# Attention, two MoE layers on one core: blocks 0 and 1 take turns with each chunk of w1 and w2, block 1's products wait in DRAM, attention's scaling moves into the masking

## The chip, the cores and the metric

One core of a Trainium2 chip. The metric is device time in microseconds of one execution; beside it stand one profiled execution and its trace.

## The reference, cut to what matters

```python
# attention: q, k, v are [4, 8, 576, 64]; heads 0-3 plain, 4-7 dilated by 4
scores = q @ k.T / sqrt(64)
scores = where(mask, scores, -1e9)          # window 32 (plain) or 128 in steps of 4 (dilated)
attn = exp(scores - max(scores)); attn = attn / (sum(attn) + 1e-9)
x = (attn @ v) as [2304 tokens, 512]
# first MoE
x = ((x @ w1) * (x @ w2)) @ w3 @ w_out      # w1, w2 [512, 1024], w3 [1024, 1024], w_out [1024, 512]
# second MoE
h = x @ w_in                                # [512, 2048]
y = (P(h) / (Q(h) + 1e-6)) @ w_out2         # P cubic, Q quadratic in h
```

The inputs of both MoE layers are float64; everything else is float32.

## The kernel before, in words

**Weights.** They come as pairs of 32-bit words (512 KB for a chunk of 128 x 512 numbers, `load`). Each chunk is decoded to float32 by one instruction of ScalarE (`scale`) and three of VectorE (`shift`, `sign`, `low_bits`). For the exact products a number is split in a high and a low part of fp32r: ScalarE rounds the high part (`high`), VectorE subtracts for the low part (`low`), and a product takes three matmuls (`SPLIT`).

**First MoE.** w3 @ w_out is made first, in two halves of 16 jobs (`w3_mm`, two matmuls of 512 columns each; "w3 job" below); its result stays as `W3o`. The 2304 tokens are eight blocks of 288 (k = 0 to 7). For block k and chunk m (0 to 7) two jobs of twelve matmuls of 288 columns make x @ w1 and x @ w2 (`l1`, e = 0 and 1), ScalarE copies the first (`l1_copy`), VectorE multiplies (`l1_mul`, the product p), ScalarE rounds p to its high part (`l1_high`) and GpSimd subtracts (`l1_low`). Eight jobs of twelve matmuls per block then multiply by W3o (`l2`). Each of the 16 chunks of w1 and w2 (two for each m) is decoded and split once, before its first l1 job; from then on all of them stay in SBUF. l1 of block 0 is thus the stage that runs while they are decoded.

**Attention.** A batch feeds two blocks and has eight groups G (four pairs of heads, two halves of the rows each). A group is a chain over the engines: scores on TensorE (`att_qk`), masking with the row maximum on VectorE (`att_mask`, six instructions, and one that scales the maxima by -0.125), six exps on ScalarE (`att_exp`), sums and reciprocal on VectorE (`att_sums`), two scalings on GpSimd (`att_norm`), transposes on TensorE (`att_pt`), copies on ScalarE (`att_pc`), the product with v on TensorE (`att_pv`), and the split into `xs` (`att_high`, `att_low`).

**Order.** All of attention and the first MoE are jobs of a planner (`Plan`). Each job has an engine, a work time, buffers and a due time; `main_jobs` writes down in which order TensorE's large jobs fall due (`PACE`, `W3_AT`), attention's groups are due some microseconds apart ahead of the first l1 job of their blocks (`GAP0`, `GAP`). The planner lists the jobs of each engine in one fixed order, and on the chip each engine takes its list in that order; an instruction that waits holds up all that stand behind it on its engine. SyncE issues all DMAs in a planned order too. PSUM has four tags of two banks: `ab` (l1), `acc` (l2, w3), `sc` (scores, second half of w3), `px` (transposes and pv). The second half of w3 needs the two `acc` banks that the first half leaves and the two `sc` banks that the last scores leave.

**Second MoE.** `phase2`, a loop written by hand. Its 32 weight chunks are decoded during the first MoE and wait in DRAM (`wd`).

Of the kernel before, what the change touches and what calls it, by code (L numbers as in the profile page):

```python
# [10 lines left out]
F32 = mybir.dt.float32  # L11
# [42 lines left out]
GAP0, GAP = 4.0, 8.0  # L54
LEAD = 20.0
W3_AT = 0
NORM_ACT = 0
PP_POOL = 0
PACE = 1.17
# [14 lines left out]
class Plan:  # L74
# [105 lines left out]
class Kern:  # L180
# [161 lines left out]
    def att_exp(self, G, h):  # L342
        pr, sm = self.pr[G], self.sm[G]
        for i in range(3 * h, 3 * h + 3):
            self.nc.scalar.activation(out=pr[:, i], in_=pr[:, i], func=AF.Exp, scale=0.125,  # L345
                                      bias=sm[:, 1, i:i + 1], accum_out=sm[:, 2, i:i + 1])

    def att_sums(self, G):
        sm = self.sm[G]
        self.nc.vector.tensor_scalar(out=sm[:, 3], in0=sm[:, 2], scalar1=1.0, scalar2=1e-9,  # L350
                                     op0=ALU.mult, op1=ALU.add)
        self.nc.vector.reciprocal(out=sm[:, 3], in_=sm[:, 3])  # L352

# [32 lines left out]
    def att_x(self, G):  # L386

        u, half = divmod(G, 2)
        b, hp = divmod(u, HP)
        if hp < HP // 2:  # L390
            return [(self.xs[2 * b + half][:, :, hp], self.xt[G][:, 0:TA])]
        sv = self.xt[G][:, 0:TA].rearrange("p (r i) -> p r i", r=2)
        return [(self.xs[2 * b + e][:, :, hp].rearrange("p w (i r) -> p w r i", r=4)
                 [:, :, 2 * half:2 * half + 2], sv[:, :, e * 72:(e + 1) * 72]) for e in range(2)]

    def att_high(self, G):
        b = G // (2 * HP)
        for k in (2 * b, 2 * b + 1):
            if k not in self.xs:
                pool = self.xs01 if k % 4 < 2 else self.xs23  # L400
                self.xs[k] = pool.tile([P, 2, KC, TA], F32R, tag=f"xs{k % 4}", bufs=1, name="xs")
        for dst, src in self.att_x(G):
            self.nc.scalar.copy(dst[:, 0], src)

    def att_low(self, G):
        for dst, src in self.att_x(G):
            self.nc.vector.tensor_tensor(out=dst[:, 1], in0=src, in1=dst[:, 0].bitcast(F32),
                                         op=ALU.subtract)
# [21 lines left out]
    def l1(self, k, m, e):  # L430
        xs, w = self.xs[k], self.w12[2 * m + e]["w"]
        t = self.ab[k, m, e] = self.bank("ab")
        n = 0
        for s in SPLIT:
            for c in range(KC):
                self.nc.tensor.matmul(t[:, 0:TA], w[:, s[0], c * P:(c + 1) * P], xs[:, s[1], c],  # L436
                                      start=n == 0, stop=n == 11)
                n += 1
# [59 lines left out]
    def phase1(self):  # L498
# [9 lines left out]
        for t in slots + [f"xs{i}" for i in range(4)]:  # L508
            bufs[t] = 1
# [12 lines left out]
        for G in range(2 * B * HP):  # L522
# [17 lines left out]
            m1 = add("DVE", 0.86, self.att_mask, G, 1, after=[qk, m0], use=[prb, smb, sc[1]])  # L540
# [3 lines left out]
            eng = "ACT" if G < NORM_ACT else "POOL"  # L544
            no = [add(eng, {"ACT": 1.2, "POOL": 0.8}[eng], self.att_norm, G, h, eng, after=[su],
                      use=[prb, smb]) for h in range(2)]
            pc = []
            for h in range(2):
# [4 lines left out]
            n = 1 if hp < HP // 2 else 2  # L553
            xn = [xsb[2 * b], xsb[2 * b + 1]]
            first = G % (2 * HP) == 0
            hi = add("ACT", 0.43 * n, self.att_high, G, after=[pv] + ([low[G - 1, "h"]] if not first else []),
                     new=xn if first else [], use=px[2:] + ([] if first else xn))
            low[G, "h"] = hi
            low[G] = add("DVE", 0.42 * n, self.att_low, G, after=[hi], use=px[2:] + xn,
                         due=due)  # L560
# [69 lines left out]
        l1s, l2s, stored = [], {}, {}  # L630
        for k in range(NA):
            b = k // 2
            lows_k = [low[G] for G in range(b * 2 * HP, (b + 1) * 2 * HP)]
            pl_lo, gbs = [], []
            for m in range(M1):
                tb = [buf("t"), buf("t")]
                mm = []
                for e in range(2):
                    ab = buf("ab")
                    mm.append((add("PE", 1.57, self.l1, k, m, e, after=lows_k + [w12[2 * m + e]] + l1s[-1:],  # L640
                                   new=[ab], use=[xsb[k], w12b[2 * m + e]], due=T["l1", k, m, e]), ab))
                    l1s.append(mm[-1][0])
                c = add("ACT", 0.42, self.l1_copy, k, m, after=[mm[0][0]], new=tb[0:1], use=[mm[0][1]],
                        due=T["l1", k, m, 1])
                mu = add("DVE", 0.42, self.l1_mul, k, m, after=[c, mm[1][0]], new=tb[1:2],
                         use=[tb[0], mm[1][1]], due=T["l1", k, m, 1] + 2)
                if m % 2 == 0:
                    gb = buf("g")
                    gbs.append(gb)
                hi = add("ACT", 0.45, self.l1_high, k, m, after=[mu], new=[gb] if m % 2 == 0 else [],  # L650
                         use=[tb[1]] + ([gb] if m % 2 else []), due=T["l1", k, m, 1] + 5)
                on_pool = k >= PP_POOL
                pl_lo.append(add("POOL" if on_pool else "DVE", 0.8 if on_pool else 0.38, self.l1_low, k, m,
                                 on_pool, after=[hi], use=[tb[1], gb], port=True))
            if k == NA - 1:
                break
# [13 lines left out]
            l1s.append(l2s[k, KC - 1])  # L670

# [34 lines left out]
    def main_jobs(self):  # L706
# [193 lines left out]
    def run(self):  # L900
        with self.pool("cpool") as self.cpool, self.pool("decp") as self.decp, \
# [3 lines left out]
            self.wd = dram.tile([2, FC, P, DM], F32, name="wd")  # L905
            self.x2d = dram.tile([2, KC, P, NT], F32, name="x2d")
# [86 lines left out]
```

## Time and profile before

| | |
|---|---|
| time, median of 3 runs | 870.48 us (869.77 to 871.95) |
| the profiled execution | 869.54 us, its span 867.8 us |
| TensorE busy in the span | 840.2 us, 97% |
| VectorE, ScalarE, GpSimd busy | 584.3, 534.0, 334.8 us |
| mean granted clock of TensorE | 0.996 of 2.4 GHz |
| DMA | 92.70 MB, mean 107 GB/s, 357 GB/s at the start |

The span runs from the first to the last instruction; the profiled time is 1.7 us more, and the median 0.9 us above the profiled time. Matmuls overlap, so a busy TensorE is not a TensorE at its peak: how long a job takes is read from the distance of its start to the next one's.

### The profile page before, as it was taken

How to read it: one execution, taken by the hardware profiler on the slowest of the kernel's cores; microseconds unless marked ns; L12 is line 12 of the kernel's file. 1: busy time of each engine (PE TensorE's matmuls, PEld its weight loads, DVE VectorE, ACT ScalarE, POOL GpSimd, SP SyncE). 2: the span in 40 equal slices, each digit the busy share in tenths (PEclk: the TensorE clock that was granted, in tenths of full speed). 3: DMA queues.
4: the chain of work that ended last, by engine and by line, in shares of the span. 5: the costliest groups of instructions: out<-in, count | busy, mean ns of one | idle time of the engine just before them, and what ended most of it. 6: DMA issues, size and time to landing. Idle time of an engine off the chain costs nothing.

```text
span 867.8 us, 14594 instructions
## 1 busy us (share of the span) xinstructions
PE 840.2 (97%) x5216; PEld 719.5 (83%) x5216; DVE 584.3 (67%) x1308; ACT 534.0 (62%) x1222; POOL 334.8 (39%) x313
## 2 busy tenths in 40 slices
PE   6989799999999999999999999999999999999998
PEld 3546599989998999989998878888888888888886
DVE  6999996776767224331214887787787877797775
ACT  5874565654566334542235877787777777787773
POOL 2220032422243222312022755565555655564443
PEclk9999999999999999999999999999999999999999
DMA  9876438585766212033225100010000100000112
GB/s 357 300 271 215 154 114 264 172 244 197 252 197 194 76 36 95 20 113 138 80 58 203 37 13 12 13 49 13 25 12 25 37 13 12 13 25 35 47 48 92
DMA packets 41737, 92.70 MB, mean 107 GB/s; under 512 B 4544, under 2 KB 12736, under 8 KB 41664
## 3 DMA queue, kind: packets, MB, share of 16 engines
q1 hardware_dynamic: 41664, 91.77, 31.7%
q8 instruction: 41, 0.67, 0.3%
q14 instruction: 32, 0.26, 0.1%
HBM read 70.39 MB, written 21.36 MB: 106 GB/s over the span
## 4 chain that ended last, share of the span: by engine, by line
PE 78%; DVE 9%; ACT 6%; DMA 4%; issue 2%; POOL 1%; SPq 0%; POOLq 0%; DVEq 0%; ACTq 0%
PE ab L436 19%; PE acc L824 11%; PE sc L824 11%; PE ab L774 11%; PE px L774 10%; PE acc L466 9%; ACT pr L345 2%; PE acc L416 2%; DVE dec L225 2%; PE sc L318 2%; PE px L383 2%; DMA words<-moe_w_in 2%; PE px L368 1%; DVE dec L236 1%; DVE dec L221 1%
## 5 line engine op out<-in xcount | busy, mean ns | idle before, releaser
L436 PE MATMUL ab<-xs,w 128*128 128x288 f32 x1536 | 216.5, 300 | 3.3 <-ACT w L243 2.8
L436 PEld LDWEIGHTS ab<-xs,w 128*128 128x128 f32 x1536 | 207.7, 190 | 8.3 <-ACT w L243 3.6
L785 POOL TENSOR_TENSOR y<-y,v 128x512 f32<-128x512 f32 x72 | 95.9, 1332 | 142.9 <-ACT y L784 142.7
L458 POOL TENSOR_TENSOR pp<-p,pp 128x288 fp32r<-128x288 f32 x64 | 55.8, 873 | 185.1 <-ACT pp L453 175.8
L361 POOL TENSOR_TENSOR pr<-pr,sm 96x384 f32<-96x384 f32 x64 | 55.2, 881 | 154.4 <-DVE sm L352 115.0
L466 PE MATMUL acc<-pp,w 128*128 128x288 f32 x768 | 110.4, 299 | 1.6 <-DVE XS L882 1.0
L824 PE MATMUL acc<-w,gg 128*128 128x512 f32 x432 | 109.8, 391 | 1.5 <-ACT r L795 1.5
L824 PE MATMUL sc<-w,gg 128*128 128x512 f32 x432 | 109.4, 390 | 0.0
L466 PEld LDWEIGHTS acc<-pp,w 128*128 128x128 f32 x768 | 103.4, 188 | 4.0 <-PE acc L466 1.2
L774 PE MATMUL ab<-XS,w 128*128 128x512 f32 (+1 forms) x480 | 105.4, 370 | 0.0
L774 PE MATMUL px<-XS,w 128*128 128x512 f32 (+1 forms) x480 | 105.3, 370 | 0.0
L811 POOL TENSOR_TENSOR gg<-t,gg 128x512 fp32r<-128x512 f32 x72 | 93.8, 1303 | 10.6 <-ACT gg L810 10.1
L774 PEld LDWEIGHTS px<-XS,w 128*128 128x128 f32 x480 | 83.9, 188 | 16.4
L774 PEld LDWEIGHTS ab<-XS,w 128*128 128x128 f32 x480 | 83.8, 188 | 16.2
L824 PEld LDWEIGHTS acc<-w,gg 128*128 128x128 f32 x432 | 80.8, 188 | 19.2 <-ACT r L795 1.9
L824 PEld LDWEIGHTS sc<-w,gg 128*128 128x128 f32 x432 | 80.9, 188 | 17.2
L446 DVE TENSOR_TENSOR p<-a_sb,ab 128x288 f32<-128x288 f32 x64 | 29.0, 453 | 88.1 <-PE ab L436 70.8
L345 ACT ACTIVATE pr<-pr,sm 96x128 f32<-96x128 f32 x192 | 74.7, 392 | 16.4 <-DVE sm L339 16.3
L802 DVE SCALAR_TENSOR_TENSOR v<-y,cs,r 128x512 f32<-128x512 f32 x72 | 71.3, 991 | 0.0
L217 ACT ACTIVATE dec<-words 128x512 f32<-128x512 f32 x72 | 47.7, 676 | 29.3 <-DMA words<-moe_w_out 9.8
L453 ACT CAST pp<-p 128x288 fp32r<-128x288 f32 x64 | 27.7, 432 | 59.2 <-DVE p L446 59.0
L794 ACT ACTIVATE r<-y,cs 128x512 f32<-128x512 f32 x72 | 52.3, 726 | 14.8 <-POOL y L785 14.7
(75 smaller groups left out, 1188.2 us busy)
## 6 DMA issues: line engine op xcount, KB each, us to landing
words<-moe_w SPq DMA_DIRECT2D x32, 512.0 KB, 5.2
words<-moe_w_out SPq DMA_DIRECT2D x24, 512.0 KB, 4.5
words<-moe_w_in SPq DMA_DIRECT2D x16, 512.0 KB, 4.2
wd<-dec SPq DMA_DIRECT2D x32, 256.0 KB, 2.3
c<-wd SPq DMA_DIRECT2D x32, 256.0 KB, 2.6
vb<-v SPq DMA_DIRECT2D x16, 384.0 KB, 3.7
XS<-x2d SPq DMA_DIRECT2D x6, 1024.0 KB, 7.9
kT<-k SPq DMA_DIRECT2D x16, 304.0 KB, 4.0
```

Source lines behind the costliest of these rows:

```text
L217: self.nc.scalar.activation(out=d.bitcast(F32), in_=s["words"].bitcast(F32)[:, :, 1], func=AF.Copy, scale=2.0 ** -112)
L345: self.nc.scalar.activation(out=pr[:, i], in_=pr[:, i], func=AF.Exp, scale=0.125, bias=sm[:, 1, i:i + 1], accum_out=sm[:, 2, i:i + 1])
L361: nc.gpsimd.tensor_tensor(out=pr[:, i], in0=pr[:, i], op=ALU.mult, in1=sm[:, 3, i].unsqueeze(2).to_broadcast([QT, 3, P]))
L436: self.nc.tensor.matmul(t[:, 0:TA], w[:, s[0], c * P:(c + 1) * P], xs[:, s[1], c], start=n == 0, stop=n == 11)
L458: eng.tensor_tensor(out=w[:, 1], in0=p, in1=w[:, 0].bitcast(F32), op=ALU.subtract)
L466: self.nc.tensor.matmul(acc[:, 0:TA], self.W3o[m][0][:, a, n * P:(n + 1) * P], self.p2[k, m // 2][:, c, m % 2], start=m == 0 and (a, c) == ...
L774: nc.tensor.matmul(t[:, e * nt:(e + 1) * nt], w[:, s[0], c * P:(c + 1) * P], XS[blk][:, s[1], c], start=n == 0, stop=n == 11)
L785: nc.gpsimd.tensor_tensor(out=w, in0=w, in1=v, op=ALU.mult)
L794: nc.scalar.activation(out=r, in_=yy[i][1], func=AF.Ln, bias=self.c1)
L802: nc.vector.scalar_tensor_tensor(out=v, in0=w, scalar=self.c1, in1=r, op0=ALU.add, op1=ALU.mult)
L811: nc.gpsimd.tensor_tensor(out=t[:, 1], in0=u, in1=t[:, 0].bitcast(F32), op=ALU.subtract)
L824: nc.tensor.matmul(acc[g, blk][tk], t[:, s[0], j:j + P], w[:, s[1]], start=f + e == 0 and s == (0, 0), stop=f + e == FG - 1 and s == (1, 0))
```

## The change

Blocks 0 and 1 now go through l1 together: for each m the four jobs (0, m, 0), (0, m, 1), (1, m, 0), (1, m, 1) follow each other. Then comes l2 of block 0, then l2 of block 1. The products of block 1 are not split when they are made. Each is stored to a DRAM tensor `pd` (`p_store`, eight of 144 KB); after l2 of block 0 has used its split products, four loads of 288 KB bring them back into the same buffers (`p_load`), ScalarE rounds (`p_high`) and VectorE subtracts (`p_low`). Half of w3's second half (W3_AT = 4) is due before the first l1 job, the rest between the chunks. The input of a batch is one tile `xs` of 576 tokens where there were two of 288, so the dilated heads' `att_high` and `att_low` are one instruction each, not two. In the masking the scale of -0.125 is an operand of the instruction, with a minimum in place of the maximum, and the instruction that scaled the maxima is gone. Two constants of the due times differ (GAP, PACE).

```diff
-GAP0, GAP = 4.0, 8.0
+GAP0, GAP = 4.0, 7.0
 LEAD = 20.0
-W3_AT = 0
-PACE = 1.17
+W3_AT = 4
+PACE = 1.12
...
             nc.vector.tensor_tensor_reduce(
...
-                op0=ALU.add, op1=ALU.max, scale=1.0, scalar=-3.0e38,
+                op0=ALU.add, op1=ALU.min, scale=-0.125, scalar=3.0e38,
                 accum_out=sm[:, 0, i:i + 1])
-        if h == 1:
-            nc.vector.tensor_scalar(out=sm[:, 1], in0=sm[:, 0], scalar1=-0.125, scalar2=0.0,
-                                    op0=ALU.mult, op1=ALU.add)
...
     def l1(self, k, m, e):
-        xs, w = self.xs[k], self.w12[2 * m + e]["w"]
+        xs, w, tok = self.xs[k // 2], self.w12[2 * m + e]["w"], slice(k % 2 * TA, (k % 2 + 1) * TA)
...
+    def p_store(self, m):
+        self.nc.sync.dma_start(out=self.pd[m // 2, :, m % 2], in_=self.pp[1, m])
+
+    def p_load(self, i):
+        w = self.p2[1, i] = self.gp.tile([P, 2, 2, TA], F32R, tag="g", bufs=5, name="pp")
+        self.nc.sync.dma_start(out=w[:, 1].bitcast(F32), in_=self.pd[i])
+
+    def p_high(self, i):
+        w = self.p2[1, i]
+        self.nc.scalar.copy(w[:, 0], w[:, 1].bitcast(F32))
+
+    def p_low(self, i):
+        w = self.p2[1, i]
+        self.nc.vector.tensor_tensor(out=w[:, 1], in0=w[:, 1].bitcast(F32), in1=w[:, 0].bitcast(F32),
+                                     op=ALU.subtract)
...
+            if k == 1:
+                kept[m] = add("SP", 0.45, self.p_store, m, after=[mu], use=tb[1:], due=d + 4)
...
+        def back_jobs():
+            pl, gbs = parts.setdefault(1, ([], []))
+            for i in range(M1 // 2):
+                gb = buf("g")
+                d = T["l2", 1, 0, 0] - 12 + 1.5 * i
+                a = add("SP", 0.95, self.p_load, i, new=[gb], due=d,
+                        after=[kept[2 * i], kept[2 * i + 1]] + parts[0][0][-1:])
+                a = add("ACT", 0.67, self.p_high, i, after=[a], use=[gb])
+                pl += [add("DVE", 0.72, self.p_low, i, after=[a], use=[gb], port=True)] * 2
+                gbs.append(gb)
...
+        for m in range(M1):
+            for k in range(2):
+                l1_jobs(k, m)
+        l2_jobs(0)
+        back_jobs()
+        l2_jobs(1)
...
-        jobs = w3(0, range(M1)) + l1(0, range(W3_AT))
+        jobs = w3(0, range(M1)) + w3(1, range(W3_AT))
         for i in range(M1):
-            jobs += w3(1, [i]) + (l1(0, [W3_AT + i]) if W3_AT + i < M1 else [])
-        jobs += l2(0)
-        for k in range(1, NA):
+            jobs += l1(0, [i]) + l1(1, [i]) + (w3(1, [W3_AT + i]) if W3_AT + i < M1 else [])
+        jobs += l2(0) + l2(1)
+        for k in range(2, NA):
             jobs += l1(k, range(M1)) + (l2(k) if k < NA - 1 else [])
```

What the planner makes of it is seen in TensorE's list. The first place is where the first half of w3 ends. `sc` are the scores of a group (`att_qk`), `px<-ident` its transposes (`att_pt`; x3 is half a group), `px<-pT` its product with v (`att_pv`), `acc<-x`, `ab<-x` and `sc<-x` are w3 jobs. Before:

```order
L318 MATMUL sc<-kT,qT 96x128 x6
L416 MATMUL acc<-x 128x512 x2
L383 MATMUL px<-pT,vb 64x96 x6
L368 MATMUL px<-ident,pr 128x96 x3
L416 MATMUL ab<-x 128x512 x2
L368 MATMUL px<-ident,pr 128x96 x3
L383 MATMUL px<-pT,vb 64x96 x6
L368 MATMUL px<-ident,pr 128x96 x6
L416 MATMUL acc<-x 128x512 x2
L383 MATMUL px<-pT,vb 64x96 x6
L416 MATMUL sc<-x 128x512 x2
```

Of the change:

```order
L359 MATMUL px<-ident,pr 128x96 x3
L406 MATMUL ab<-x 128x512 x2
L359 MATMUL px<-ident,pr 128x96 x3
L316 MATMUL sc<-kT,qT 96x128 x6
L374 MATMUL px<-pT,vb 64x96 x6
L316 MATMUL sc<-kT,qT 96x128 x6
L359 MATMUL px<-ident,pr 128x96 x6
L374 MATMUL px<-pT,vb 64x96 x6
L316 MATMUL sc<-kT,qT 96x128 x6
L359 MATMUL px<-ident,pr 128x96 x6
L406 MATMUL acc<-x 128x512 x2
L406 MATMUL sc<-x 128x512 x2
```

Attention's first scores used to open the list and now stand behind five w3 jobs; so three groups of the eight still have their scores to come when the first half of w3 ends (the `ab<-x` above), and eight attention steps stand in a row without a w3 job between them; before it was three.

The second place is TensorE's list around the last w3 jobs (`acc<-x`, `sc<-x`) and l1 (`ab<-xs,w`, twelve matmuls a job). Before, where four jobs of l1 had gone ahead of these rows:

```order
L416 MATMUL acc<-x 128x512 x2
L416 MATMUL sc<-x 128x512 x2
L416 MATMUL acc<-x 128x512 x2
L416 MATMUL sc<-x 128x512 x2
L416 MATMUL acc<-x 128x512 x2
L436 MATMUL ab<-xs,w 128x288 x12
L416 MATMUL sc<-x 128x512 x2
L436 MATMUL ab<-xs,w 128x288 x108
L318 MATMUL sc<-kT,qT 96x128 x6
L436 MATMUL ab<-xs,w 128x288 x24
L466 MATMUL acc<-pp,w 128x288 x12
```

Of the change, from its first l1 job on:

```order
L426 MATMUL ab<-xs,w 128x288 x48
L406 MATMUL sc<-x 128x512 x2
L426 MATMUL ab<-xs,w 128x288 x48
L406 MATMUL acc<-x 128x512 x2
L406 MATMUL sc<-x 128x512 x2
L426 MATMUL ab<-xs,w 128x288 x12
L406 MATMUL acc<-x 128x512 x2
L406 MATMUL sc<-x 128x512 x2
L406 MATMUL acc<-x 128x512 x2
L406 MATMUL sc<-x 128x512 x2
L426 MATMUL ab<-xs,w 128x288 x96
```

25 w3 jobs now stand ahead of the first l1 job, not 19, and each m brings 48 matmuls of l1, not 24.

The third place is between l2 of block 0 and l2 of block 1 (`acc<-pp,w`) on TensorE, and the loaded products on ScalarE. TensorE before, where l1 of block 1 (`ab`) goes over into its l2:

```order
L436 MATMUL ab<-xs,w 128x288 x12
L466 MATMUL acc<-pp,w 128x288 x12
L318 MATMUL sc<-kT,qT 96x128 x6
L368 MATMUL px<-ident,pr 128x96 x3
L466 MATMUL acc<-pp,w 128x288 x12
L368 MATMUL px<-ident,pr 128x96 x3
L466 MATMUL acc<-pp,w 128x288 x12
```

TensorE of the change; the x24 ends l2 of block 0, the x48 begins that of block 1:

```order
L472 MATMUL acc<-pp,w 128x288 x24
L374 MATMUL px<-pT,vb 64x96 x6
L316 MATMUL sc<-kT,qT 96x128 x6
L359 MATMUL px<-ident,pr 128x96 x6
L316 MATMUL sc<-kT,qT 96x128 x6
L374 MATMUL px<-pT,vb 64x96 x6
L316 MATMUL sc<-kT,qT 96x128 x6
L472 MATMUL acc<-pp,w 128x288 x48
```

ScalarE of the change at that place (`L340` is `att_exp`, `L459` is `p_high`, `L365` `att_pc`):

```order
L481 CAST x_1980<-acc 128x288
L365 COPY pT<-px 128x288 x2
L340 ACTIVATE pr,sm<-pr,sm 96x128 x6
L459 CAST pp<-pp 128x576 x3
L393 CAST xs<-px 128x2x144
L340 ACTIVATE pr,sm<-pr,sm 96x128 x6
```

Six attention steps stand between the two blocks' l2, and the last three `p_high` stand behind the six exps of the group whose scores are the first of the three `sc` rows.

## Rows read from the trace of the kernel before

**Rows 1.** Stages: length, busy PE, PEld, DVE, ACT, POOL (instructions), clock, DMA, GB/s.

```profile
7.94:65.81 57.87, 54.66 (x316) 29.14 (x317) 54.52 (x197) 43.84 (x152) 13.65 (x16) 0.97 0.86 314
65.81:121.86 56.05, 51.56 (x258) 37.75 (x257) 53.46 (x104) 28.73 (x57) 7.79 (x7) 0.97 0.46 151
121.86:195.82 73.96, 70.65 (x626) 65.56 (x624) 51.49 (x178) 44.09 (x159) 21.87 (x25) 1.00 0.72 227
195.82:451.78 255.96, 253.68 (x2102) 245.57 (x2101) 104.48 (x385) 113.04 (x383) 66.37 (x79) 1.00 0.37 120
```

**Rows 2.** TensorE's timeline, three places: start, length, work.

```profile
19.89 0.90 PE L318 MATMUL sc<-kT,qT 64*96 64x128 f32 x12
20.72 1.99 PE L416 MATMUL acc<-x 128*128 128x512 f32 x4
22.54 0.66 PE L368 MATMUL px<-ident,pr 96*128 96x96 f32 x6
23.04 1.91 PE L416 MATMUL ab<-x 128*128 128x512 f32 x4
24.87 0.72 PE L383 MATMUL px<-pT,vb 128*64 128x96 f32 x12
25.52 0.68 PE L318 MATMUL sc<-kT,qT 64*96 64x128 f32 x8
...
79.49 1.88 PE L416 MATMUL sc<-x 128*128 128x512 f32 x4
81.21 1.88 PE L416 MATMUL acc<-x 128*128 128x512 f32 x4
...
387.81 25.75 PE L436 MATMUL ab<-xs,w 128*128 128x288 f32 x192
413.40 12.95 PE L466 MATMUL acc<-pp,w 128*128 128x288 f32 x96
```

**Rows 3.** TensorE's waits from 65.81 to 121.86: total us, times, longest.

```profile
PE ab L436 <- ACT w L243: 2.8, 1, 2.8
PE acc L416 <- DVE x L236: 1.7, 1, 1.7
```

**Rows 4.** TensorE and its granted clock behind the longest of these waits.

```profile
101.40:108.00 6.60, 6.54 (x36) 0.74 0.23 89
```

**Rows 5.** VectorE's timeline: masking, two decodes at once, product, low part.

```profile
20.82 0.29 DVE L334 CUSTOM_DVE_ANT_0 pr<-sc,masks 96x128 f32<-96x128 f32 x1
...
22.28 0.75 DVE L221 TENSOR_SCALAR dec<-dec 128x512 int32<-128x512 int32 x2
...
25.36 0.42 DVE L221 TENSOR_SCALAR dec<-dec 128x512 int32<-128x512 int32 x1
...
69.69 0.46 DVE L446 TENSOR_TENSOR p<-a_sb,ab 128x288 f32<-128x288 f32 x1 [0.90 <-PE ab L436]
70.06 0.68 DVE L247 TENSOR_TENSOR w<-dec,w 128x512 fp32r<-128x512 f32 x1
70.66 0.68 DVE L225 SCALAR_TENSOR_TENSOR dec<-words,dec 128x512 int32<-128x512 int32 x1
71.38 1.18 DVE L236 SCALAR_TENSOR_TENSOR x<-words,dec 128x512 int32<-128x512 int32 x1
```

**Rows 6.** TensorE's timeline at the last group of the first batch.

```profile
54.28 0.38 PE L383 MATMUL px<-pT,vb 128*64 128x96 f32 x2
...
58.35 3.60 PE L416 MATMUL acc<-x 128*128 128x512 f32 x4
```

**Rows 7.** ScalarE's exps, by line, up to 130 us.

```profile
L345 ACT ACTIVATE pr<-pr,sm 96x128 f32<-96x128 f32 x61 | 23.8, 393 | 4.6 <-DVE sm L339 4.6
```

**Rows 8.** GpSimd's timeline beside the last row of rows 5.

```profile
70.69 1.32 POOL L458 TENSOR_TENSOR pp<-p,pp 128x288 fp32r<-128x288 f32 x1 [13.26 <-ACT pp L453]
```

**Rows 9.** TensorE's longest waits from 121.86 to 195.82, then from 195.82 to 451.78.

```profile
PE px L368 <- POOL pr L361: 2.0, 3, 1.4
...
PE px L368 <- POOL pr L361: 2.0, 2, 1.6
```

More of the change, by code (lines that the diff above doesn't have):

```diff
@@ L389, in att_x @@
         b, hp = divmod(u, HP)
+        x, r = self.xs[b][:, :, hp], self.xt[G][:, 0:TA]
         if hp < HP // 2:
[L391 to L394, printed above, removed]
+            return x[:, :, half * TA:(half + 1) * TA], r
+        return (x.rearrange("p w (i r) -> p w r i", r=4)[:, :, 2 * half:2 * half + 2],
+                r.rearrange("p (r i) -> p r i", r=2))
     def att_high(self, G):
         b = G // (2 * HP)
[L398 to L403, printed above, removed]
+        if b not in self.xs:
+            pool = (self.xs01, self.xs23)[b % 2]
+            self.xs[b] = pool.tile([P, 2, KC, S], F32R, tag="xs", bufs=1, name="xs")
+        dst, src = self.att_x(G)
+        self.nc.scalar.copy(dst[:, 0], src)
     def att_low(self, G):
-        for dst, src in self.att_x(G):
-            self.nc.vector.tensor_tensor(out=dst[:, 1], in0=src, in1=dst[:, 0].bitcast(F32),
-                                         op=ALU.subtract)
+        dst, src = self.att_x(G)
+        self.nc.vector.tensor_tensor(out=dst[:, 1], in0=src, in1=dst[:, 0].bitcast(F32),
+                                     op=ALU.subtract)
     def w3_mm(self, half, j, e):
@@ L507, in phase1 @@
         slots = [f"p{i}" for i in range(12)] + [f"w3{i}" for i in range(6)] + [f"wo{i}" for i in range(8)]
-        for t in slots + [f"xs{i}" for i in range(4)]:
+        for t in slots + ["xs0", "xs1"]:
             bufs[t] = 1
@@ L543, in phase1 @@
             su = add("DVE", 0.3, self.att_sums, G, after=[e0, e1], use=[smb])
[L544 to L546 removed]
+            no = [add("POOL", 0.8, self.att_norm, G, h, after=[su], use=[prb, smb]) for h in range(2)]
             pc = []
@@ L552, in phase1 @@
             pv = add("PE", 0.78, self.att_pv, G, after=pc + [lv], new=px[2:], use=[pTb, lb[2]])
-            n = 1 if hp < HP // 2 else 2
-            xn = [xsb[2 * b], xsb[2 * b + 1]]
             first = G % (2 * HP) == 0
-            hi = add("ACT", 0.43 * n, self.att_high, G, after=[pv] + ([low[G - 1, "h"]] if not first else []),
-                     new=xn if first else [], use=px[2:] + ([] if first else xn))
+            hi = add("ACT", 0.43, self.att_high, G, after=[pv] + ([low[G - 1, "h"]] if not first else []),
+                     new=[xsb[b]] if first else [], use=px[2:] + ([] if first else [xsb[b]]))
             low[G, "h"] = hi
-            low[G] = add("DVE", 0.42 * n, self.att_low, G, after=[hi], use=px[2:] + xn,
-                         due=due)
+            low[G] = add("DVE", 0.5, self.att_low, G, after=[hi], use=px[2:] + [xsb[b]], due=due)
         self.nd = 0
@@ L627, in phase1, with l1_jobs @@
             w12[j] = add("DVE", 0.64, self.low, s, after=[hi], use=[db, pb], port=True)
-        l1s, l2s, stored = [], {}, {}
-        for k in range(NA):
+        l1s, l2s, stored, parts, kept = [], {}, {}, {}, {}
+        def l1_jobs(k, m):
             b = k // 2
[L633 to L646, printed above, removed]
-                if m % 2 == 0:
[L648 to L656, printed above, removed]
@@ new lines, in l1_jobs @@
+            tb = [buf("t"), buf("t")]
+            mm = []
+            for e in range(2):
+                ab = buf("ab")
+                mm.append((add("PE", 1.57, self.l1, k, m, e, new=[ab], use=[xsb[b], w12b[2 * m + e]],
+                               after=[low[G] for G in range(b * 2 * HP, (b + 1) * 2 * HP)] +
+                               [w12[2 * m + e]] + l1s[-1:], due=T["l1", k, m, e]), ab))
+                l1s.append(mm[-1][0])
+            d = T["l1", k, m, 1]
+            c = add("ACT", 0.42, self.l1_copy, k, m, after=[mm[0][0]], new=tb[0:1], use=[mm[0][1]], due=d)
@@ new lines, in l1_jobs @@
+            mu = add("DVE", 0.42, self.l1_mul, k, m, after=[c, mm[1][0]], new=tb[1:2],
+                     use=[tb[0], mm[1][1]], due=d + 2)
+            if k == 1:
+                kept[m] = add("SP", 0.45, self.p_store, m, after=[mu], use=tb[1:], due=d + 4)
+            else:
+                pl, gbs = parts.setdefault(k, ([], []))
+                if m % 2 == 0:
+                    gbs.append(buf("g"))
+                hi = add("ACT", 0.45, self.l1_high, k, m, after=[mu], new=gbs[-1:] if m % 2 == 0 else [],
+                         use=[tb[1]] + (gbs[-1:] if m % 2 else []), due=d + 5)
+                pl.append(add("POOL", 0.8, self.l1_low, k, m, after=[hi], use=[tb[1], gbs[-1]]))
@@ L657, in phase1, with l2_jobs @@
+        def l2_jobs(k):
+            pl, gbs = parts[k]
             for n in range(KC):
@@ L670, in phase1 @@
             l1s.append(l2s[k, KC - 1])
+        for m in range(M1):
[5 more added lines that the diff above has]
+        for k in range(2, NA):
+            for m in range(M1):
+                l1_jobs(k, m)
+            if k < NA - 1:
+                l2_jobs(k)
         bst = []
```

41 lines of the change are left out of this document (18 added, 23 removed).

## Prediction

> **What bounds the kernel now.** I read the stages first. I cut the span where TensorE's list has the same work behind it before and after: A from the first matmul (7.94) to the first l1 job (65.81), B to the end of block 0's l1 (121.86), C to the first l1 job of block 2 (195.82), D to the second MoE (451.78). The last 416 us are the second MoE, which the diff leaves alone. TensorE is busy nearly all of every stage, but in A and B VectorE is as busy: 54.52 of 57.87 us and 53.46 of 56.05; in C and D it is not [rows 1]. So there are two candidates in A and B, and TensorE's busy time alone doesn't settle it, since records overlap.
>
> Second, the timeline gives what TensorE's work costs when nothing holds it up [rows 2]: a group's scores 0.83 (19.89 to 20.72), transposes 0.50 (22.54 to 23.04), product with v 0.65 (24.87 to 25.52), so 1.98 a group; a w3 job 1.72 (79.49 to 81.21); sixteen l1 jobs 25.59 (387.81 to 413.40), 1.60 each, and l2 jobs, also twelve matmuls of 288 columns, the same. With the jobs counted in TensorE's list:
>
> A: 19 w3 jobs and 8 groups, 48.5 us; it takes 57.87, so 9.4 are lost.
> B: 13 w3 jobs, 16 of l1, one group's scores, 48.8; takes 56.05, lost 7.25.
> C: 16 of l1, 16 of l2, 8 groups, 67.0; takes 73.96, lost 7.0.
>
> Together 164.3 of work and 23.6 lost. Only the lost time can change, for the changed list has the same 164.3 before block 2's l1, cut otherwise: A 58.8 (25 w3 jobs, 8 groups), B 70.5 (7 w3 jobs, 32 of l1, four groups less one product with v), C 35.0 (16 of l2 and the rest of the groups).
>
> Third, the waits name B's loss: TensorE waits 2.8 and 1.7 us for chunks that are still being decoded [rows 3], 4.5 together. Behind the longer wait the granted clock averages 0.74 over 6.60 us [rows 4], part of it at the lower of its two levels; that costs 0.26 x 6.60 = 1.7 more. About 1.0 is left.
>
> **The change, part by part: B.** For each m VectorE needs two decodes, 3.08 us (22.28 to 25.36), two low parts of 0.60 (70.06 to 70.66) and a product of 0.37 (69.69 to 70.06): 4.65 [rows 5]. TensorE uses them up in two l1 jobs, 3.2. VectorE sets the pace. With both blocks VectorE needs one product more, 5.0, and TensorE four jobs, 6.4. Now TensorE sets it, and decoding runs ahead. I take both waits and the low clock as gone. What stays is the 1.0, stretched to the longer stage (x 70.5 / 48.8): 1.5. And four groups of the second batch move from C into B. What C loses beside its 2.0 us of waits for GpSimd [rows 9] is 5.0 for 8 groups, 0.62 each for switching and small waits; four bring 2.5. B loses 4.0. Bounds: 2.0, and 7.25 if the chunks' waits come back elsewhere.
>
> **C.** Four groups leave, four stay: 2.5 of switching. The 2.0 for GpSimd stood between l1 and l2 of a block; that border is gone for block 1, but a new one comes: the last three loads must wait until l2 of block 0 is done with its buffers. TensorE has six attention steps there, 0.65 + 0.83 + 0.50 + 0.83 + 0.65 + 0.83 = 4.3 us [rows 2]. ScalarE's three `p_high` stand behind six exps of the group whose scores end 1.5 us in. Masking takes that group to 3.0 (20.82 to 22.28 is 1.46, [rows 5]), the exps (0.39 each, [rows 7]) to 5.3. No row shows `p_high` or `p_low` on 576 columns; a subtraction of 512 takes 0.68 [rows 5], and I take 0.7 for each, between 0.39 and the 1.3 of a GpSimd one [rows 7, 8]. So l2 of block 1 can begin at 6.7, a wait of 2.4. The loads have those 5.3 us to land; they cost nothing unless they take longer, and then one for one; a load that waits in SyncE's list also holds up the word loads behind it, for which nobody waits in C. The eight stores stand among the last w12 loads in SyncE's list, behind products that TensorE's pace sets; B has more than 1 us of slack for each m, so I cost them at nothing.
>
> To this comes GpSimd. The sums that stand just ahead of the three `p_low` on VectorE start two of its scalings. The trace shows what such a neighbour costs: while a GpSimd subtraction ran at 70.69 for 1.32 us [rows 8], VectorE's `low_bits`, with two inputs from SBUF, took 1.18 at 71.38, where its like takes 0.68 [rows 5]: 0.5 more. Three `p_low` with two such inputs: 1.5. The Trainium skill, page "SBUF — State Buffer", section "Who interferes with whom", states that a VectorE instruction with two SBUF inputs and a GpSimd instruction that reads SBUF lock each other out, so that the later one waits for all of the earlier one. The row agrees in kind. By that rule each of the three could wait a whole 1.32, 4.0 in all, and the sum below would end 2.5 us later.
>
> With 2.4 + 1.5 = 3.9 for the new border C loses 6.4. Bounds: 2.5 (the border is hidden) and 9.
>
> **A.** More must be ready before l1: six more w3 jobs on TensorE (10.3 us), and in VectorE's list 25 decodes, not 20, ahead of the batch's last low part. VectorE's load grows from 54.52 to 54.52 + 5 x 1.54 + 0.6 = 62.8, TensorE's work from 48.5 to 58.8; if VectorE never waited, A would still lose about 4. Against it stands the list: eight attention steps in a row, where each waits for its chain. The last group of the batch shows such exposure before: 54.28 to 58.35, 4.07 us for 1.15 of work (a product with v and transposes), 2.9 lost [rows 6]. I take the same 9.4 as before: a better balance, a worse order. Bounds: 4, and more in the rivals.
>
> **The small edits.** The scaling instruction goes from the end of the masking: six masks and it take 1.46 together, so it is at most some 0.3 [rows 5]; eight in A are at most 2.4 on VectorE, hidden behind TensorE's row of attention steps, taken as 0. One `att_high` and `att_low` in place of two for dilated heads: on neither bound, 0; where VectorE bounds A they count with that bound.
>
> **D.** The same work. Before, TensorE waits 2.0 us for GpSimd, 1.6 of it at once, where l1 of a block goes over into l2 with transposes close behind scores [rows 9]. At that place the new list has three l2 jobs (4.8 us) ahead; I take 1.6 off. Bounds: 0 and 2, and a loss of 2 if the groups, now due 7 apart, crowd.
>
> **Sum.** A 0; B 7.25 - 4.0 = 3.25 less; C 7.0 - 6.4 = 0.6 less; D 1.6 less: 5.45. The profiled execution took 869.54, so 864.1; the median stands 0.94 above it, so 865.0.
>
> **The rivals.** (1) *The front falls into place.* VectorE alone bounds A, it loses 4, not 9.4: 865.0 - 5.4 = 859.6, or 858.5 with the scaling's time. For it: VectorE was 94% busy in A. Against: the eight steps. (2) *`p_low` locked out*, each of the three for a whole GpSimd instruction of 1.32 us and not for 0.5 [rows 5, 8]: + 2.5, 867.5. For it: the sums start the scalings just then. Against: a `p_low` may well start first. (3) *Two groups more exposed in A*: + 2 x 2.9 = 870.8, no change. (4) *Slower: all four groups of the row exposed*, each waiting as the last one did: + 4 x 2.9, and a stretch at low clock as in B, + 1.7: 878.3. It decides from three on, for 5.45 + 2.6 = 8.1. For it: three groups have their scores still to come when the first half of w3 ends, and the second half can't begin before their banks are free. Against: their chains overlap each other, and before there was only one group left to overlap.
>
> **How the numbers follow.** 0.3% of 870 is 2.6 us, about what a measurement of this kernel can tell from no change. Forecast 0.51 (861 to 867.8), (1) 0.14, (2) 0.10, half of it within 2.6 us of before, (3) 0.15, (4) 0.10. Faster 0.51 + 0.14 + 0.05 = 0.70, the same 0.20, slower 0.10. The range from 858.5 (A at its lower bound) to 871 (two groups exposed) leaves out (4) and some of the edges.
>
> **What would show it.** B: no wait of TensorE for `high` or `low_bits`, and clock 1.00 in l1 of blocks 0 and 1. A: first l1 job near 7.9 + 58.8 + 9.4 = 76; 71 speaks for (1), 82 for (3). C: a wait of 2 to 5 us before l2 of block 1, put down to `p_low`. First l1 job of block 2 near 192. The prediction is wrong if A loses over 17, if waits for chunks stay in B, or if TensorE waits for `l1_mul` in it.

## The result and the profile after

The changed kernel takes 861.57 us (median of 4 runs, 860.87 to 862.43) against 870.18 for the kernel before beside it: ratio 0.9898, 95% interval 0.988 to 0.9915. The forecast was 865.0 with a range from 858.5 to 871. The gain is 8.6 us, where the sum said 5.45.

The stages of the profiled execution after, in the columns of [rows 1]; the last row is the second MoE:

```profile
7.94:77.50 69.56, 65.96 (x340) 34.13 (x341) 60.66 (x198) 46.66 (x153) 15.18 (x16) 0.98 0.83 301
77.50:149.49 71.99, 71.99 (x523) 63.18 (x521) 65.05 (x159) 42.46 (x118) 15.26 (x16) 1.00 0.52 168
149.49:190.02 40.53, 37.97 (x340) 34.58 (x338) 30.34 (x108) 26.72 (x93) 9.68 (x10) 1.00 0.82 270
190.02:443.38 253.36, 253.15 (x2103) 244.93 (x2101) 102.18 (x355) 112.92 (x366) 62.98 (x77) 1.00 0.39 128
443.38:859.10 415.72, 409.66 (x1922) 341.25 (x1920) 317.40 (x443) 301.62 (x469) 221.99 (x171) 1.00 0.12 40
```

Block 2's first l1 job comes at 190.02 and not at 195.82 (5.8 less), D takes 253.36 for 255.96 (2.6 less), the second MoE 0.3 less: 8.7 of the span. Against the work that the prediction counted, A loses 69.56 - 58.8 = 10.8, B 71.99 - 70.5 = 1.5, C 40.53 - 35.0 = 5.5.

TensorE's waits, first in A, then in C; for B the view has no row at all, where [rows 3] stood before:

```profile
PE acc L406 <- DVE x L234: 8.7, 1, 8.7
PE px L359 <- POOL pr L352: 1.7, 2, 1.3
PE sc L316 <- DVE sm L332: 1.0, 2, 0.7
...
PE px L359 <- DVE xs L397: 1.3, 2, 0.9
PE sc L316 <- DVE sm L332: 1.0, 3, 0.6
PE acc L472 <- DVE pp L463: 0.2, 1, 0.2
```

The first of them is the start, before A. The others of A stand in the row of attention steps. TensorE's timeline at the start of A and at the row, and, from the windows, the granted clock behind it:

```profile
8.72 3.78 PE L406 MATMUL acc<-x 128*128 128x512 f32 x4 [8.72 <-DVE x L234]
12.30 2.40 PE L406 MATMUL ab<-x 128*128 128x512 f32 x4
14.54 1.88 PE L406 MATMUL acc<-x 128*128 128x512 f32 x4
...
47.50 0.41 PE L359 MATMUL px<-ident,pr 96*128 96x96 f32 x3
...
50.81 0.89 PE L316 MATMUL sc<-kT,qT 64*96 64x128 f32 x10 [0.71 <-DVE sm L332]
...
53.59 1.11 PE L316 MATMUL sc<-kT,qT 64*96 64x128 f32 x12
56.04 0.47 PE L359 MATMUL px<-ident,pr 96*128 96x96 f32 x3 [1.34 <-POOL pr L352]
...
57.13 3.10 PE L406 MATMUL acc<-x 128*128 128x512 f32 x4
60.03 2.43 PE L406 MATMUL sc<-x 128*128 128x512 f32 x4
62.29 1.88 PE L406 MATMUL acc<-x 128*128 128x512 f32 x4
...
50.00:56.00 6.00, 3.81 (x41) 2.85 (x40) 5.96 (x28) 6.00 (x25) 2.44 (x4) 1.00 0.90 311
58.00:60.00 2.00, 2.00 (x3) 0.67 (x2) 1.93 (x6) 2.00 (x11) 0.20 (x1) 0.50 0.99 401
60.00:62.00 2.00, 2.00 (x5) 0.97 (x4) 0.45 (x3) 2.00 (x11) 1.41 (x2) 0.72 0.89 301
```

From 50 to 56 TensorE is busy 3.81 of 6 us; two microseconds later its clock is at the lower level, 1.2 GHz, and a w3 job takes 2.90 (57.13 to 60.03), the next 2.26 (to 62.29), where one in [rows 2] takes 1.72. That is 1.7 us for the low clock. The row itself, from 47.50 to 57.13, takes 9.63 for 5.04 of work by the prices of [rows 2]: 4.6 lost, of which the waits name 2.9. And the first two w3 jobs take 3.58 and 2.24 (8.72, 12.30, 14.54), 2.4 more than two of 1.72; the clock column says 1.00 there, so why they are slow stays open.

At the border in C: TensorE's timeline, VectorE's (one `p_low` by itself at 154.65, three together), GpSimd's (two scalings by themselves, two beside the `p_low`):

```profile
165.65 0.72 PE L374 MATMUL px<-pT,vb 128*64 128x96 f32 x12
...
172.71 2.98 PE L472 MATMUL acc<-pp,w 128*128 128x288 f32 x20
175.93 2.25 PE L472 MATMUL acc<-pp,w 128*128 128x288 f32 x15 [0.24 <-DVE pp L463]
...
154.65 0.75 DVE L463 TENSOR_TENSOR pp<-pp 128x576 fp32r<-128x576 f32 x1
172.51 3.36 DVE L463 TENSOR_TENSOR pp<-pp 128x576 fp32r<-128x576 f32 x3 [0.17 <-ACT pp L459]
...
159.24 1.61 POOL L352 TENSOR_TENSOR pr<-pr,sm 96x384 f32<-96x384 f32 x2 [11.76 <-DVE sm L347]
172.51 2.75 POOL L352 TENSOR_TENSOR pr<-pr,sm 96x384 f32<-96x384 f32 x2 [6.07 <-ACT pp L459]
```

The six attention steps take 7.06 (165.65 to 172.71) for 4.3 of work, then l2 of block 1 begins and waits only 0.24 for `p_low`. The neighbours pay for each other: the two scalings take 2.75 for 1.61, the three `p_low` 3.36 where the kernel of experiment 12 below, with no scaling beside them, takes 2.09:

```profile
169.51 2.09 DVE L463 TENSOR_TENSOR pp<-pp 128x576 fp32r<-128x576 f32 x3 [0.66 <-ACT pp L459]
```

But nearly all of this passes while l2 of block 1 is already running on the products that are ready.

### The profile page after: what moved, and what is told of

It is laid out like the page before. It is cut to its first block, busy times and chain, and to the rows that moved or that the text cites. A ratio compares the mean times of both kernels' runs of the same rounds, so it can differ in the third digit from the quotient of the medians.

```text
span 859.1 us, 14509 instructions
## 1 busy us (share of the span) xinstructions
PE 838.7 (98%) x5216; PEld 718.1 (84%) x5216; DVE 578.5 (67%) x1264; ACT 533.7 (62%) x1202; POOL 328.1 (38%) x305
## 4 chain that ended last, share of the span: by engine, by line
PE 89%; ACT 5%; DVE 4%; DMA 1%; issue 1%; POOL 0%; SPq 0%; ACTq 0%; POOLq 0%; DVEq 0%
PE ab L426 24%; PE acc L851 11%; PE sc L851 11%; PE ab L801 11%; PE px L801 10%; PE acc L472 10%; PE acc L406 3%; PE sc L316 2%; PE px L374 2%; PE sc L406 2%; PE px L359 2%; PE ab L406 1%; DMA words<-moe_w_in 1%; ACT pr L340 1%; DVE v L829 1%
## 5 line engine op out<-in xcount | busy, mean ns | idle before, releaser
L447 POOL TENSOR_TENSOR pp<-p,pp 128x288 fp32r<-128x288 f32 x56 | 48.1, 860 | 162.7 <-ACT pp L443 156.1
L340 ACT ACTIVATE pr<-pr,sm 96x128 f32<-96x128 f32 x192 | 74.8, 395 | 9.0 <-DVE sm L332 9.0
L821 ACT ACTIVATE r<-y,cs 128x512 f32<-128x512 f32 x72 | 52.2, 726 | 14.5 <-POOL y L812 14.3
L811 ACT ACTIVATE y<-v,cs 128x512 f32<-128x512 f32 x72 | 58.8, 817 | 2.4
```

What stands on the lines that cost most here:

```text
L811: nc.scalar.activation(out=w, in_=v, func=AF.Identity, scale=self.b1, bias=self.b0)
L821: nc.scalar.activation(out=r, in_=yy[i][1], func=AF.Ln, bias=self.c1)
```

## The experiments

Each is the changed kernel with one edit, where nothing else is said. Ratios are to runs of the kernel before on the same chip; the brackets are 95% intervals. The changed kernel itself stands at 0.9898 [0.988, 0.9915].

**1. The turns undone.** Edit: `main_jobs` and the job loops as before (block 0's jobs mixed with w3's second half), `W3_AT = 0`, block 1 split as all others:

```diff
-            if k == 1:
+            if k == -1:
                 kept[m] = add("SP", 0.45, self.p_store, m, after=[mu], use=tb[1:], due=d + 4)
...
-        jobs = w3(0, range(M1)) + w3(1, range(W3_AT))
+        jobs = w3(0, range(M1)) + l1(0, range(W3_AT))
```

> Blocks 0 and 1 no longer take turns: block 0's twelve-matmul jobs are mixed with the second half of w3 as before, block 1 comes after l2 of block 0, its products stay split in SBUF, nothing goes through DRAM. Attention's scaling in the masking, the xs tile of a whole batch and the planner's new distances (7.0, 1.12) stay as in the changed kernel (861.6). Theory (the turns bring the gain before block 2): up to the first l1 job of block 2 the gain of 5.8 us is lost again, TensorE waits for high and low_bits in l1 of block 0 as before (4 to 5 us); 866 to 868. Rival (the scaling and the xs tile bring it, by VectorE's time in stage A): 861 to 863.

864.23 us (861.45 to 867.64), ratio 0.9933 [0.9908, 0.9958]. The wait for chunks in block 0's l1 is back, and the low clock behind it; waits from 63.87 to 120.99, then windows of this profile (which was the slowest execution of the six):

```profile
PE ab L426 <- ACT w L241: 3.8, 1, 3.8
...
98.00:106.00 8.00, 5.72 (x24) 5.72 (x25) 7.66 (x14) 3.63 (x7) 1.31 (x1) 0.57 0.12 47
136.00:140.00 4.00, 3.31 (x14) 3.31 (x15) 1.95 (x13) 2.51 (x13) 2.51 (x4) 0.57 0.92 298
```

In this execution block 2's first l1 job comes at 195.97, as late as before. So the mechanism stands, but the median is between theory and rival: 2.7 us of the 8.6 go with the turns, 6 stay, and the interval touches that of the changed kernel.

**2. Old distances.** Edit: `GAP = 8.0`, `PACE = 1.17`.

> The changed kernel with the planner's old distances for attention's groups of the later batches (8.0 for 7.0) and its old pace (1.17 for 1.12). Theory (stage D gained its 2.6 us because GpSimd's lows and the transposes no longer meet at the border of l1 and l2, which hangs on where the groups fall, so on these two numbers): D loses 2 us or more again, with waits for GpSimd in it; 863.5 to 864.5. Rival (D gained from the groups that the turns moved ahead, or from the scaling's instruction that is gone): 861 to 862, D within 0.7 of 253.4.

861.56 us (861.1 to 862.51), 0.9902 [0.9879, 0.9925]: no difference. The theory fell: D takes 254.65, 1.3 more, and block 2's l1 starts at 189.35, 0.7 earlier.

**3. No chunk of w3's second half ahead.** Edit: `W3_AT = 0`.

> The changed kernel with none of the second half of w3 ahead of l1 (0 chunks for 4): eight w3 jobs move from before the first l1 job to between the jobs of blocks 0 and 1. Theory (with two blocks TensorE has 6.4 + 3.4 us of work for each m in B, VectorE 5.0 + 1.5, so decoding still runs ahead; A gets shorter, and the row of eight attention steps is gone): first l1 job at 60 to 66, no wait for chunks in B, 858 to 861. Rival (without a start VectorE's decoding is again too late for l1 of block 0, and the waits for high and low_bits come back, 3 to 5 us): 864 to 867.

865.99 us, 0.9946 [0.9926, 0.9966], but not for the rival's reason: B has no wait at all, so decoding keeps up with two blocks even without a start. What it lost is the front. The list now begins with scores, and TensorE's waits up to the first l1 job (66.75) say so; the first w3 job starts at 13.4, not 8.7:

```profile
PE acc L406 <- DVE x L234: 5.5, 3, 3.9
PE sc L316 <- DMA qT<-q: 4.8, 1, 4.8
PE px L374 <- ACT pT L365: 1.3, 2, 0.9
```

A low clock at the end of A (0.63 from 64 to 68) and in C (0.57 from 172 to 180) came on top, some 1.5 and 3.4 us in this execution.

**4. Attention earlier.** Edit: `GAP0 = 8.0`.

> The changed kernel with the groups of the first batch due 8.0 apart and not 4.0, so that they stand earlier in all lists and no row of eight attention steps is left in A (four at most). Theory (A loses 10.8 us because of the row: its waits for GpSimd and masks of 2.7 us and 1.7 at low clock behind it): A loses 6 to 7, 857 to 858. Rival (VectorE bounds A; what attention doesn't wait for, the w3 jobs wait for, as its decodes come later): A loses 10 to 12, 861 to 863.

863.88 us, 0.9926 [0.9907, 0.9944]. First l1 job at 83.5: the same loss at the front, greater (first w3 job at 17.8, 6.4 us of waiting for q). It doesn't test the row by its time, since the row was broken up at the price of the start. Its trace shows, though, that the four steps left in a row still pay: one wait of 2.9 for the scalings, and a stretch at low clock (0.50 from 60 to 66; the w3 jobs from 62.33 on take 3.46 and 2.15).

**5. Only the scaling, in the kernel before.** Edit: the scaling's instruction out, the masks as in the change; lists as before.

> The kernel before, with attention's scaling done in the masking and its own instruction gone; every other instruction stands where it stood, since the planner's cost of the masking is left at 0.86. It tells what the removed instruction itself is worth. Theory (it is hidden, as the prediction had it, or worth a few tenths where VectorE holds the front up): 869 to 870.5. Rival (the first experiment, which lost the turns but kept 6 us of the gain, owes that to this instruction; 32 groups with 0.17 to 0.78 us on VectorE each): 864 to 866.

867.85 us (11 runs), 0.9979 [0.9963, 0.9994]: between the two, about 1.8 us by the ratio, not nothing. D takes 254.66 where [rows 1] has 255.96:

```profile
195.04:449.70 254.66, 253.64 (x2102) 245.54 (x2101) 100.86 (x369) 113.20 (x383) 66.09 (x79) 1.00 0.37 120
```

**6. Scaling and the xs tile, old order, old distances.** Edit: those of 1 and 2 together.

> The kernel before with the scaling in the masking, the masking's new cost of 0.66 for the planner and the xs tile of a whole batch; no turns, no DRAM, old distances (8.0) and pace (1.17). Theory (what the first experiment kept came from these edits, above all from the lists that the planner writes with the new costs; the distances bring nothing, as the second experiment showed): 863 to 866. Rival (the new distances brought it with the old order): 869 to 871.

870.28 us (11 runs, 865.87 to 874.14), 0.9994 [0.997, 1.0018]. The rival holds. Without the turns the two distances decide over 5.3 us (0.9994 to 0.9933); with them, over nothing (0.9902 to 0.9898). The turns are worth 0.0092 or 8.0 us at the old distances, 3.0 at the new ones (there the intervals touch). Against 5 (0.9979), the xs tile and the planner's new work times (0.66 for the second half of the masking, less for the split into `xs`) bring nothing that can be told; neither was tried by itself.

**7. The scaling back.** Edit (the masks are again those of the kernel before, maximum and scale 1.0, and the exps' scale is 0.125):

```diff
+        if h == 1:
+            nc.vector.tensor_scalar(out=sm[:, 3], in0=sm[:, 0], scalar1=-0.125, scalar2=0.0,
+                                    op0=ALU.mult, op1=ALU.add)
...
-                                      bias=sm[:, 0, i:i + 1], accum_out=sm[:, 1, i:i + 1])
+                                      bias=sm[:, 3, i:i + 1], accum_out=sm[:, 1, i:i + 1])
```

> The changed kernel with attention's scaling as an instruction of its own again, one for each group, all lists otherwise as they are. Theory (hidden): 861.5 to 862.5. Rival (VectorE's time in A counts one for one, eight instructions of 0.17 to 0.78 there): 863 to 866.

865.09 us (862.41 to 865.84), 0.9945 [0.9925, 0.9964]: the rival's size, but not its place: 3.5 us more, 4.1 by the ratio. A is as long as without it (first l1 job at 77.7); C and D pay, 1.3 and 2.5:

```profile
150.00:191.84 41.84, 37.99 (x339) 34.55 (x338) 30.40 (x112) 26.54 (x93) 9.44 (x10) 1.00 0.82 264
191.84:447.68 255.84, 254.53 (x2102) 245.23 (x2101) 105.10 (x370) 112.21 (x366) 62.82 (x77) 1.00 0.39 127
```

The masks themselves take as long as in the changed kernel, 281 ns each. What grows is ScalarE's idle time ahead of the exps, over the whole run, first in the changed kernel, then here:

```profile
L340 ACT ACTIVATE pr<-pr,sm 96x128 f32<-96x128 f32 x192 | 74.8, 395 | 9.0 <-DVE sm L332 9.0
L343 ACT ACTIVATE pr<-pr,sm 96x128 f32<-96x128 f32 x192 | 74.7, 393 | 25.2 <-DVE sm L337 25.2
```

**8. No sign.** Edit: the body of `sign` is `pass`; decoded chunks lose their sign.

> The changed kernel without the instruction that sets the sign in each decoded chunk (0.67 us on VectorE, left out for all chunks, all lists otherwise as they are). It asks what bounds A. Theory (VectorE: 25 decodes are needed before the first l1 job, 16.7 us less for it): the first l1 job comes 6 to 9 us earlier than 77.5, near 8 + 59 + 3 = 70, nothing more to gain in B; 853 to 856. Rival 1 (the row of attention's exposed chains): first l1 job at 75 to 77. Rival 2 (the loads of the 512 KB chunks, as the DMA engines are busy 0.83 of A): first l1 job at 75 to 77 too, with waits for words ahead of the scalings on ScalarE in place of VectorE's work.

857.08 us (2 runs), 0.9859 [0.9835, 0.9882]. A and B:

```profile
7.70:73.50 65.80, 63.48 (x340) 33.09 (x341) 46.16 (x173) 46.55 (x154) 14.14 (x16) 1.00 0.85 320
73.50:145.50 72.00, 72.00 (x523) 63.19 (x521) 51.08 (x139) 42.46 (x118) 15.36 (x16) 1.00 0.52 169
```

B stays as long (72.00 for 71.99) with 14 us less on VectorE: in B TensorE sets the pace, shown. A begins 1.0 earlier (7.70 against 8.72) and ends 4.0 earlier, so it gets 3.0 shorter, 1.7 of it the low clock that is gone. VectorE's 14.5 us less in A bring a fifth of that, not all of it; the theory was too strong. The first l1 job, at 73.5, lies between it and both rivals. ScalarE's waits for words up to there grow, from 8.3 to 11.7, so the loads (rival 2) aren't excluded.

**9. Nothing comes back.** Edit: `p_load` gives block 0's parts to l2 of block 1, `p_high` and `p_low` do nothing; the output of block 1 is that of other products.

> The changed kernel without the way back of block 1's products: the four loads, p_high and p_low are left out, l2 of block 1 takes block 0's parts instead (the stores stay, all lists are otherwise as they are). It measures what the border in C costs. Theory (the border costs what the prediction gave it, a bit less than 3.9: six attention steps of 4.3 us take 7.1 there, and p_low runs beside GpSimd's scalings): C falls from 40.5 to 37 to 38.5; 858.5 to 860. Rival (the six steps wait for their own chains, and p_high and p_low are hidden behind them): C stays above 39.5; 860.5 to 862.

861.57 us, 0.9875 [0.9848, 0.9902] (the kernel before at 873.06 on this chip, as for 10 and 11). C takes 39.31; below it stands TensorE's timeline at the border:

```profile
148.97:188.28 39.31, 37.62 (x340) 34.62 (x339) 25.87 (x104) 24.33 (x89) 8.17 (x10) 1.00 0.77 249
...
165.13 0.72 PE L374 MATMUL px<-pT,vb 128*64 128x96 f32 x12
...
172.70 6.67 PE L468 MATMUL acc<-pp,w 128*128 128x288 f32 x48
```

The six attention steps take 7.57 (165.13 to 172.70) with nothing to wait for behind them: the border is attention's own. The whole way back costs 1.2 us in C, nothing that the time shows. Nearer to the rival.

**10. One instruction less in the sums.** Edit:

```diff
-        self.nc.vector.tensor_scalar(out=sm[:, 2], in0=sm[:, 1], scalar1=1.0, scalar2=1e-9,
-                                     op0=ALU.mult, op1=ALU.add)
-        self.nc.vector.reciprocal(out=sm[:, 2], in_=sm[:, 2])
+        self.nc.vector.reciprocal(out=sm[:, 2], in_=sm[:, 1])
```

> The changed kernel with one instruction less between the exps and the scalings of each group: the 1e-9 that is added to the sums of exps is left out (each sum holds an exp of 0, so it is at least 1 and the addition changes no bit of it), the reciprocal reads the sums at once. 32 instructions of 0.17 us alone, all lists otherwise as they are. The scaling's instruction, as short and in the same chain, was worth 2 to 3.5 us in two experiments. Theory (a short VectorE instruction in attention's chain is paid at many places, for GpSimd, TensorE's transposes and l2 stand behind it): 859 to 860.5. Rival (what cost time was only the scaling's place ahead of the exps): 861 to 862.3.

861.39 us (859.11 to 862.08), 0.9864 [0.9841, 0.9888]: no difference that can be told from the changed kernel. The rival.

**11. The scaling there, but unread.** Edit: the instruction of 7, the masks and the exps unchanged.

> The changed kernel with the scaling's instruction back in VectorE's list where it stood, but nobody reads what it writes: the exps still take what the masking leaves. Theory (its price is the chain from the masks to the exps, which is then as short as without it): 861.5 to 862.5. Rival (its price is VectorE's own time and the waiting for GpSimd in front of what stands behind it): 864 to 866, as with the scaling back.

862.08 us (861.64 to 863.09), 0.9878 [0.9858, 0.9899]; the interval of 7 lies wholly above it. VectorE has the instruction's time again, at no cost that can be told from none (0.5 us more, by the ratio less). ScalarE's idle time ahead of the exps is 8.3 us, not the 25.2 of 7. So its price in 7 is that the exps wait for it. (7 and 11 ran on different chips, and their runs just overlap in microseconds. The profiled execution of 11 has 41.53 in C, but with a stretch at low clock in it, 0.69 from 174 to 178, and 254.61 in D, half-way between the changed kernel and 7.)

**12. Two chunks ahead.** Edit: `W3_AT = 2`.

> The changed kernel with two chunks of the second half of w3 ahead of l1 (2 for 4). In its list the w3 jobs still come first, as the front of the changed kernel has it and the third and fourth experiment had not, and attention's steps stand one group to two w3 jobs, with no row of eight. Theory (B has slack on VectorE, so less needs to be decoded ahead; and without the row A loses neither its 2.7 us of waits for scalings and masks nor the 1.7 at low clock): first l1 job at 68 to 71, no wait for chunks in B, first l1 job of block 2 at 186.5 to 188.5, 858 to 860. Rival (VectorE bounds the whole front, so what A gives B takes, and the waits for high and low_bits come back): first l1 job of block 2 at 190 or later, 861.5 to 865.

858.11 us (856.68 to 858.93), 0.9841 [0.9821, 0.9861], below the changed kernel's whole interval. A to D:

```profile
8.70:66.12 57.42, 56.61 (x325) 29.92 (x325) 51.77 (x185) 43.42 (x148) 13.71 (x16) 1.00 0.85 314
66.12:145.10 78.98, 78.98 (x539) 66.23 (x537) 72.75 (x173) 45.84 (x123) 14.51 (x16) 1.00 0.59 197
145.10:187.24 42.14, 38.87 (x354) 35.31 (x352) 31.78 (x111) 27.63 (x95) 9.10 (x10) 1.00 0.81 270
187.24:440.60 253.36, 252.77 (x2088) 244.21 (x2087) 101.35 (x349) 111.94 (x363) 64.20 (x77) 1.00 0.37 123
```

The clock is 1.00 in all four, and the place of the row looks like this, w3 jobs between the groups:

```profile
47.95 1.98 PE L406 MATMUL acc<-x 128*128 128x512 f32 x4
49.77 0.66 PE L359 MATMUL px<-ident,pr 96*128 96x96 f32 x6
50.26 1.91 PE L406 MATMUL ab<-x 128*128 128x512 f32 x4
...
52.75 0.90 PE L316 MATMUL sc<-kT,qT 64*96 64x128 f32 x12
53.92 0.47 PE L359 MATMUL px<-ident,pr 96*128 96x96 f32 x3 [0.27 <-POOL pr L352]
...
56.31 1.98 PE L406 MATMUL acc<-x 128*128 128x512 f32 x4
...
169.53 0.53 PE L472 MATMUL acc<-pp,w 128*128 128x288 f32 x2 [1.29 <-ACT pp L459]
```

TensorE's list has 21 w3 jobs and 8 groups ahead of the first l1 job, 52.0 of work; from its first matmul A takes 57.42 and loses 5.4, where the changed kernel, counted so too (from 8.72), loses 10.0. One group in a row is left there, 3.56 (52.75 to 56.31) for 1.98 of work. B has no wait for chunks. C is 1.6 longer than in the changed kernel, with 1.1 more of attention's work in it; here l2 of block 1 does wait for the way back, 1.3 for `p_high` (the last row) and 0.3 for `p_low`. Block 2's l1 starts 2.8 us earlier than in the changed kernel. The theory holds; only the first l1 job is earlier than it said.

## Why the prediction was right, and where it wasn't

**B** was right in its mechanism. With two blocks TensorE sets the pace (8), the chunks' waits go and come back with the old order (1), and two blocks have the slack even without a start (3, 12). Its size was too high: 1.5 lost where 4.0 were forecast, as if the four groups that moved in had brought none of the 2.5 for switching; B shows no wait at all.

**C** lost 5.5 (forecast 6.4), with a wrong picture of the border: the announced wait of 2 to 5 us for `p_low` is 0.24. The neighbours' price was sized well: 3.36 - 2.09 = 1.3, forecast 1.5. But it isn't on the path: l2 of block 1 goes through the products in their order; it starts on those of the first load, which had a free buffer early (the `p_low` at 154.65), and reaches the last ones 0.24 us before they are ready. What fills the border is attention's own chain, 2.8 us over its work, and 3.3 with nothing coming back (9). The way back costs 1.2 (9), not 3.9; in another list it can come onto the path (12). Rival (2) priced each `p_low` at a GpSimd instruction of 1.32, but that one had itself been lengthened beside VectorE (its like takes 0.80 by itself, at 372.65 in the kernel before); a scaling takes 0.8, and only two stood there. By the rule of the Trainium skill (page "SBUF — State Buffer", section "Who interferes with whom") that the later of the two waits for all of the earlier one, three `p_low` and two scalings in turn need 2.09 + 1.61 = 3.70 us, an estimate from their times alone. They took 3.36, so the trace agrees to within 0.34.

**D** gained 2.6 (forecast 1.6), at least half of it for another reason. I put it down to the three l2 jobs ahead of the first groups, which were to end the waits for GpSimd. But with the scaling back, in the same lists, these waits are gone as well, and D takes 255.84; in the kernel before without the scaling it takes 254.66 [rows 1 for 255.96]; in the kernels of 9 to 11, where the exps don't wait for a scaling, 254.4 to 254.6. So 1.3 to 2.5 of the 2.6 hang on it, each read from one execution. The lists count too: in 6, without the scaling but with the old order and distances, D takes 257.34.

**The small edits** are the step that failed: "taken as 0". The scaling's instruction is worth 1.8 us in the kernel before (5) and 3.5 in the changed one (7), on the path from the masks to the exps (11) and outside A. I had only bounded its time on VectorE, 0.3 each, and asked whether VectorE was the bound, not who stood behind it. (The range's lower end takes 1.1 us for it, for which no row is given; the bound beside it is 2.4.) The new distances, which I mentioned only as a risk for D, are worth 5.3 us without the turns and nothing with them (6).

**A** lost 10.8 (forecast 9.4), 0.8 of it since TensorE's first matmul comes at 8.72 and not at 7.94. The order was the lever, as "a worse order" said: counted from the first matmul A loses 10.0, and a list without the row 5.4 (12), though with four w3 jobs less ahead of l1. The 10.0 are 4.6 in the row, 1.7 at low clock, 2.4 in the first two w3 jobs (in 12 the same) and 1.3 elsewhere. Of the 11.6 that rival (4) feared for four groups, the row cost 4.6, and one low clock came behind it as it said.

So the time came 3.4 us under the forecast by misses of both signs: the forecast was 1.4 too low in A and 2.5, 0.9 and 1.0 too high in B, C and D. That they cancel in part is luck. The edits don't add up to 8.6: the scaling alone 1.8 to 3.5, the turns 3.0 to 8.0, distances 0 to 5.3, each by what the others are. What stays open: which places in D carry the scaling's price, for TensorE's waits name 1.2 of the 1.3 in C but only 0.9 of the 2.5 in D, why the first w3 jobs are slow, and what sets the length of A beside the row (VectorE by a fifth, 8; the loads weren't tested).

## What to carry to other kernels

A short instruction on a slack engine can cost far more than its own time when another engine's chain stands behind it (7), or nothing (10): ask who waits for it, not what share its engine has. When a planner writes the lists, an edit's neighbours in the list can be worth more than the edit; hold the lists fixed to price an instruction (5, 7, 10, 11), and try the planner's numbers by themselves (2, 3, 6, 12). And interleave: here one chain to two long jobs cost less (12) than the same chains in a row, which paid twice, by the waits and by the clock behind them.

## What was not expected of the hardware

Executions of one kernel differ in part by how often the clock falls: the six of experiment 1 run from 861.45 us at a mean granted clock of 0.998 to 867.64 at 0.992, those of experiment 12 from 856.68 at 1.000 to 858.93 at 0.997. It isn't all: in 7 the fastest, 862.41, has 0.997 and the slowest, 865.84, has 0.998. And the clock fell without a long idle time just before: in the changed kernel the longest wait between the start and the fall is 1.34 us, in a stretch where TensorE was busy 3.81 of 6.
